# One 128-partition load for the shifted values, gate rows patched from Pool's queue, and a new issue order

## Chip, cores, metric

The kernel runs on one core of a Trainium2 chip. The metric is the device time of one execution in microseconds, lower is better. Before the change the median was 159.94 us over four runs (157.32 to 165.34).

Executions of one kernel vary by a few per cent here. A run over 1.5% above the fastest of the same kernel is called slow, and ratios are taken from fast runs alone.

## The reference

A layer norm, then two branches on the same normalised rows: a sliding attention with 32 heads of 20 channels, where each position looks at 8 keys that lie 2 apart, and a gate, in which a router picks 2 of the 2048 rows, an expert MLP changes those two, and a SiLU of the result multiplies the attention output.

```python
def reference(A_x, A_wqkv, A_wo, B_x, B_w_r, B_w_gate, B_w_up, B_w_down):   # cut
    x = A_x                                  # (1, 2048, 640) bf16
    xn = _layernorm(x, axis=-1)
    # A: W, dil = 8, 2;  idx = pos[:, None] - arange(W) * dil, masked where negative
    #    logits = q . k[idx] * scale; attn = softmax(logits); o = attn . v[idx]; s = o @ wo
    # B: r = xn @ w_r; idx = argsort(-r)[:, :2]; y = (silu(xs @ w_gate) * (xs @ w_up)) @ w_down
    #    y *= sigmoid(r[idx]); upd = scatter_add(0, idx, y); returns xn + upd
    s = _A_ref(xn, A_wqkv, A_wo)
    g = _silu(_B_ref(xn, B_w_r, B_w_gate, B_w_up, B_w_down))
    return x + s * g
```

## The kernel before

The sequence is worked in four stages of 512 positions. The values of a stage go to a scratch in device memory (`vd`) and come back as `vsh`, where partition 32·w4 + h holds head h shifted by 2·w4 positions. VectorE multiplies them with the attention weights (`av`), TensorE sums the products. There is one `vsh` for all stages, so a part of it can be loaded for the next stage only when this stage's product has read it.

```python
def load_wo(dd):                              # four loads of 32 partitions
    src = bass.AP(A_wo.tensor, A_wo.offset + dd * D, [[DH * D, H], [4 * D, G5], [1, D]])
    nc.sync.dma_start(wo[32 * dd:32 * (dd + 1), :, :], src)

def v_load(j, g0, ng):                        # called with (0, 2), (2, 2), (4, 1): 12 DMAs a stage
    n = (4 * ng - 1) * VR + ST + 8            # 4202 or 2098 elements a row
    for w4 in range(4):
        src = bass.AP(vd[j].tensor, vd[j].offset + 4 * g0 * VR + HALO - 8 - DIL * w4, [[DH * VR, H], [1, n]])
        nc.sync.dma_start(vsh[32 * w4:32 * (w4 + 1), 4 * g0 * VR:4 * g0 * VR + n], src)

def av(j, u):                                 # cut: one product over a part of vsh
    nc.vector.tensor_tensor(out=dst, in0=attn..., in1=vv, op=ALU.mult)

def gate_out():                               # the two 128-row tiles that hold the picked rows, to scratch
    for k in range(2):
        src, dst = gate_tile(k)
        nc.sync.dma_start(out=dst, in_=src)
def gate_rows():                              # the two new rows into the scratch
    for k in range(2):
        nc.sync.dma_start(out=zd[bass.ds(regs[k], 1), :]..., in_=grow[k:P:32, :])
def gate_back():                              # and the tiles back
    for k in range(2):
        dst, src = gate_tile(k)
        nc.sync.dma_start(out=dst, in_=src)

# ... cut; every engine runs its own steps in the order of one hand-made list, ORDER:
# zo, zw, zi = gate_out, gate_rows, gate_back; vs = store values; vl = load vsh; y = av;
# cm = combine (result times gate); od = add it to the output
for name in ORDER.split():
    step[name]()
```

All of these DMAs but the `od` ones of the first three stages (Pool's queue) stand on the sync queue, which issues them in this order. While one of them waited, none behind it was issued: in the trace of the kernel before, the second of `zo` waited 8.5 us for the first, and the vsh loads behind it went out from 99.9 us on only.

## Time and profile before

| | before |
|---|---|
| median of 4 runs | 159.94 us |
| profiled execution (slow) | 163.1 us span, granted clock 0.93 |
| TensorE (PE) / VectorE (DVE) / ScalarE (ACT) busy | 83% / 75% / 67% |

Lines of the page of the kernel before: busy time, the DMA engines' busy tenths in 40 slices, the chain of waits that ended last, one group of instructions (busy us, mean ns, idle time before it and what ended it), and one group of DMA issues (count, KB each, median us from issue to landing).

```profile
span 163.1 us, 3011 instructions
...
PE 135.0 (83%) x1159; PEld 66.9 (41%) x1179; DVE 122.0 (75%) x118; ACT 108.6 (67%) x201; POOL 17.7 (11%) x77
...
DMA  5899994098999033999995862993668999921175
...
PE 54%; DMA 27%; ACT 5%; DVE 5%; SPq 4%; issue 2%; DVEq 0%
PE pp L284 31%; PE so L421 9%; DMA vsh<-vd 8%; DMA wg<-in_B_w_gate_dram 7%; DMA zd<-grow 5%; PE lg L333 4%; DMA vd<-v_sb 3%; PE oa L407 3%; PE tp L274 3%; DMA z<-in_A_x_dram 2%; SPq L314 2%; DMA z<-zd 2%; DVE ss L467 1%; SPq L486 1%; DVE pr
...
L392 DVE TENSOR_TENSOR prod<-attn,vsh 128x8192 bf16<-128x8192 bf16 (+3 forms) x14 | 44.6, 3202 | 13.4 <-DMA vsh<-vd 13.1
...
vsh<-vd SPq DMA_DIRECT2D x32, 262.6 KB, 8.5
```

TensorE rules the first two thirds. VectorE's product L392 sat idle 13.4 us, nearly all of it for vsh, and all of that after 110 us, in the tail of the kernel. A 262.6 KB load takes 8.5 us at the median, with several in flight.

Windows of the kernel before (start and end; length; busy us and count of each engine; granted clock, DMA share of 16 engines, GB/s; up to 20 packet records are open at once in the first window, so that a share can read above 1). The first, second and last windows hold mostly vsh loads, the third wg (weights, 128 rows), the fourth mostly wd (weights, 108 rows).

```profile
core 0: us, PE busy (x) PEld busy (x) DVE busy (x) ACT busy (x) POOL busy (x), PEclk, DMA share, GB/s
43.00:51.00 8.00, 7.88 (x73) 4.69 (x77) 8.00 (x7) 7.96 (x15) 0.00 (x0) 1.00 1.02 224
64.00:76.00 12.00, 11.89 (x100) 5.40 (x100) 9.81 (x13) 9.97 (x15) 3.76 (x3) 1.00 1.00 225
80.50:82.50 2.00, 2.00 (x11) 0.91 (x10) 2.00 (x1) 1.07 (x2) 0.00 (x0) 1.00 1.10 342
92.00:96.00 4.00, 3.95 (x33) 2.27 (x33) 3.83 (x6) 3.93 (x7) 0.00 (x0) 1.00 0.83 237
126.00:138.00 12.00, 6.85 (x60) 2.96 (x61) 6.63 (x5) 4.89 (x9) 2.34 (x2) 0.76 1.04 235
```

Two things to read. With the DMA engines full (shares of 1.00 to 1.10), vsh loads move only 224 to 235 GB/s, wg 342. And wd's 108-row loads keep the engines 83% busy from 92 to 96 us. No record names the engine of a packet; the count of engines is read from such shares.

What the sync queue waited for in the kernel before (us in total, times, longest), then pieces of its chain of waits (start, length, what):

```profile
SPq L314 <- DMA vd<-v_sb: 12.0, 3, 4.3
...
SPq L593 <- DMA zd<-z: 8.5, 1, 8.5
SPq L597 <- DMA zd<-grow: 7.9, 1, 7.9
...
SPq L602 <- DMA z<-zd: 1.8, 1, 1.8
```

```profile
104.54 8.60 DMA zd<-grow
...
116.11 2.54 DMA z<-zd
...
119.08 5.30 DMA vd<-v_sb
...
125.77 5.89 DMA vsh<-vd
...
131.68 7.66 DMA vsh<-vd
```

The row patches of the gate hold the sync queue from 104.5 us; the last stage's value store is issued at 119.1 only, and its shifted loads land at 139.

### The profile page before, as it was taken

The numbers are of one execution on the slowest core, as the hardware profiler recorded it, in microseconds if no ns is written. First come the engines' busy times: TensorE is split into PE (matmuls) and PEld (weight loads), VectorE is DVE, ScalarE is ACT, GpSimd is POOL, SyncE is SP. The second block draws the span as 40 slices with busy tenths as digits, with TensorE's granted clock in tenths as the row PEclk, the third lists the DMA queues.
The fourth block names the chain that finished last, engine by engine and source line by source line (L and its number), as shares of the span: only waits on it lengthen the run. The fifth ranks groups of instructions, "written<-read, shape, count | busy, mean of one in ns | idle before, by whom it ended". The sixth has DMA issues, their size and how long they took to land.

```text
span 163.1 us, 3011 instructions
## 1 busy us (share of the span) xinstructions
PE 135.0 (83%) x1159; PEld 66.9 (41%) x1179; DVE 122.0 (75%) x118; ACT 108.6 (67%) x201; POOL 17.7 (11%) x77
## 2 busy tenths in 40 slices
PE   6779999999999999999969999993199619499630
PEld 2256545434455434444424636341063303165410
DVE  1635299999999999599988898932799365794930
ACT  3987998998799999977679879954025721145100
POOL 7880000000000000161000000000000303000110
PEclk9969999999999999999999999999659975969995
DMA  5899994098999033999995862993668999921175
GB/s 152 209 375 368 302 329 155 10 316 214 285 227 305 16 131 111 245 206 214 333 330 142 256 200 73 227 225 62 172 182 242 220 234 242 191 41 44 41 127 114
DMA packets 18958, 32.08 MB, mean 197 GB/s; under 512 B 2192, under 2 KB 16720, under 8 KB 17872
## 3 DMA queue, kind: packets, MB, share of 16 engines
q1 hardware_dynamic: 17072, 29.60, 67.0%
q0 software_dynamic: 1584, 1.97, 7.6%
q10 hardware_dynamic: 288, 0.33, 0.6%
q8 instruction: 9, 0.15, 0.4%
q14 instruction: 5, 0.04, 0.1%
HBM read 26.24 MB, written 7.61 MB: 208 GB/s over the span
## 4 chain that ended last, share of the span: by engine, by line
PE 54%; DMA 27%; ACT 5%; DVE 5%; SPq 4%; issue 2%; DVEq 0%
PE pp L284 31%; PE so L421 9%; DMA vsh<-vd 8%; DMA wg<-in_B_w_gate_dram 7%; DMA zd<-grow 5%; PE lg L333 4%; DMA vd<-v_sb 3%; PE oa L407 3%; PE tp L274 3%; DMA z<-in_A_x_dram 2%; SPq L314 2%; DMA z<-zd 2%; DVE ss L467 1%; SPq L486 1%; DVE prod L392 1%
## 5 line engine op out<-in xcount | busy, mean ns | idle before, releaser
L284 PE MATMUL pp<-xnT,wqkv 128*128 128x512 bf16 (+1 forms) x302 | 68.6, 373 | 0.7
L392 DVE TENSOR_TENSOR prod<-attn,vsh 128x8192 bf16<-128x8192 bf16 (+3 forms) x14 | 44.6, 3202 | 13.4 <-DMA vsh<-vd 13.1
L322 DVE TENSOR_TENSOR prod<-q_sb,k_sb 128x4096 bf16<-128x4096 bf16 (+1 forms) x14 | 44.4, 3193 | 2.8 <-ACT k_sb L299 2.4
L284 PEld LDWEIGHTS <-wqkv 128*128 128x128 bf16 x315 | 30.2, 99 | 33.8 <-issue 3.2
L421 PE MATMUL so<-wo,o_sb 128*128 128x128 bf16 (+1 forms) x153 | 27.5, 339 | 2.4 <-DVE ss L467 1.4
L407 PE MATMUL oa<-prod,sall 128*32 128x512 bf16 (+2 forms) x240 | 12.7, 327 | 12.5 <-DVE prod L392 11.6
L421 PEld LDWEIGHTS <-o_sb 128*128 128x128 bf16 x160 | 14.7, 114 | 14.6 <-issue 7.5
L441 ACT CAST ss<-so 128x512 bf16<-128x512 f32 x12 | 7.0, 601 | 17.0 <-PE so L421 10.6
L417 ACT CAST o_sb<-oa 128x512 bf16<-128x512 f32 (+2 forms) x22 | 11.8, 564 | 7.2 <-PE oa L407 4.8
L292 ACT ACTIVATE q_sb<-pp 128x512 bf16<-128x512 f32 (+1 forms) x23 | 12.4, 545 | 4.4 <-PE pp L284 4.4
L299 ACT CAST v_sb<-pp 128x512 bf16<-128x512 f32 x20 | 11.6, 589 | 4.2 <-PE pp L284 4.0
L458 POOL DMA_DIRECT2D out_dram<-ss x3 | 4.0, 1341 | 77.3 <-DVE ss L455 77.3
L407 PEld LDWEIGHTS <-sall 128*32 128x32 bf16 x240 | 4.9, 98 | 18.4 <-issue 9.5
L247 DVE BATCH_NORM_STATS2 st<-z 128x6 f32<-128x320 bf16 x16 | 7.0, 478 | 6.7 <-DMA z<-in_A_x_dram 6.7
L299 ACT CAST k_sb<-pp 128x512 bf16<-128x512 f32 x20 | 11.4, 588 | 0.5 <-PE pp L284 0.5
L278 ACT COPY xnT<-tp 128x640 bf16<-128x640 bf16 x16 | 10.5, 705 | 0.7 <-PE tp L274 0.7
L333 PE MATMUL lg<-prod,ind 128*32 128x512 bf16 x160 | 10.2, 380 | 0.1
L476 ACT ACTIVATE z<-z 128x1280 bf16<-128x1280 bf16 x8 | 10.3, 1285 | 0.0
L162 ACT ACT_TABLE_LOAD x7 | 9.0, 1283 | 1.9 <-PEq L696 1.8
L274 PE MATMUL tp<-ident,z 128*128 128x128 bf16 x80 | 7.2, 231 | 2.0 <-DVE z L268 2.0
L274 PEld LDWEIGHTS <-z 128*128 128x128 bf16 x80 | 5.5, 103 | 5.5 <-DVE z L268 2.9
L268 DVE TENSOR_SCALAR z<-z,mv,rstd 128x640 bf16<-128x640 bf16 x16 | 6.5, 454 | 1.0 <-ACT rstd L264 1.0
(88 smaller groups left out, 103.4 us busy)
## 6 DMA issues: line engine op xcount, KB each, us to landing
vsh<-vd SPq DMA_DIRECT2D x32, 262.6 KB, 8.5
vd<-v_sb SPq DMA_DIRECT2D x4, 657.5 KB, 4.3
wqkv<-in_A_wqkv_dram SPq DMA_DIRECT2D x3, 800.0 KB, 8.6
wu<-in_B_w_up_dram SPq DMA_DIRECT2D x5, 432.0 KB
wg<-in_B_w_gate_dram SPq DMA_DIRECT2D x5, 432.0 KB, 10.7
wd<-in_B_w_down_dram SPq DMA_DIRECT2D x4, 540.0 KB
vsh<-vd SPq DMA_DIRECT2D x16, 131.1 KB, 3.0
z<-in_A_x_dram SPq DMA_DIRECT2D x3, 640.0 KB, 12.2
```

The lines of the kernel that those rows point to most:

```text
L274: nc.tensor.transpose(tp[:, k5, :], z[:, i, P * k5:P * (k5 + 1)], ident[:])
L278: nc.scalar.copy(xnT[:, :, P * i:P * (i + 1)], acc.pop(("t", i))[:])
L284: nc.tensor.matmul(pp[:], lhsT=wqkv[:, k5, col:col + P], rhs=xnT[:, k5, ST * j + t0:ST * j + t0 + n], start=(k5 == 0), stop=(k5 == KD - 1))
L292: nc.scalar.activation(out=dst, in_=pp[:], func=ACT.Copy, scale=SCALE)
L299: nc.scalar.copy(dst, pp[:])
L322: nc.vector.tensor_tensor(out=dst, in0=q_sb[:, s0:s0 + n, :].unsqueeze(2).to_broadcast([P, n, W, ST]), in1=kv, op=ALU.mult)
L333: nc.tensor.matmul(lg[32 * w4:32 * (w4 + 1), w2, :], lhsT=ind5[:, g, :], rhs=prod[:, a:a + ST], start=(g == 0), stop=(g == G5 - 1), tile_p ...
L392: nc.vector.tensor_tensor(out=dst, in0=attn[:, :, t0:t0 + n].unsqueeze(2).to_broadcast([P, 2, 4 * ng, n]), in1=vv, op=ALU.mult)
L407: nc.tensor.matmul(oa[32 * dd:32 * (dd + 1), i, :], lhsT=sall[:, 0:32], rhs=prod[:, a:a + n], start=(w2 == 0), stop=(w2 == 1), tile_positi ...
L417: nc.scalar.copy(o_sb[:, s0:s0 + m, t0:t0 + n], acc.pop(("o", j, g, t0))[:])
L421: nc.tensor.matmul(dst, lhsT=o_sb[:, o_slot(j, g), P * c:P * (c + 1)], rhs=wo[:, g, n0:n1], start=(g == 0), stop=(g == G5 - 1))
L476: nc.scalar.activation(out=z[:, 2 * h:2 * h + 2, :], in_=z[:, 2 * h:2 * h + 2, :], func=ACT.Silu)
```

## The change

Four things. (V) The four loads of a group pair become one of 128 partitions, with the shifts numbered the other way round so that the source steps forward. Its evident intent is fewer issues and a destination that reaches every partition. (W) The wo weights are loaded by group, in the same form. (G) The six gate DMAs go to Pool's queue, over two scratch copies, each of which gets both rows. (O) All steps are put in a new order.

```diff
-    zd = dram.tile([S, D], BF, name="zd")
+    zd = [dram.tile([S, D], BF, name=f"zd{k}") for k in range(2)]
@@ load_wo, one per group g
-        src = bass.AP(A_wo.tensor, A_wo.offset + dd * D, [[DH * D, H], [4 * D, G5], [1, D]])
-        nc.sync.dma_start(wo[32 * dd:32 * (dd + 1), :, :], src)
+        src = bass.AP(A_wo.tensor, A_wo.offset + 4 * g * D, [[D, 4], [DH * D, H], [1, D]])
+        nc.sync.dma_start(wo[:, g, :], src)
@@ v_load
-        for w4 in range(4):
-            src = bass.AP(vd[j].tensor, vd[j].offset + 4 * g0 * VR + HALO - 8 - DIL * w4, [[DH * VR, H], [1, n]])
-            nc.sync.dma_start(vsh[32 * w4:32 * (w4 + 1), 4 * g0 * VR:4 * g0 * VR + n], src)
+        off, dst = vd[j].offset + 4 * g0 * VR + HALO - 8 - 3 * DIL, vsh[:, 4 * g0 * VR:4 * g0 * VR + n]
+        src = bass.AP(vd[j].tensor, off, [[DIL, 4], [DH * VR, H], [1, n]])
+        nc.sync.dma_start(dst, src)
@@ gate_out and gate_back: nc.sync -> nc.gpsimd, zd -> zd[k]; gate_rows:
-            nc.sync.dma_start(out=zd[bass.ds(regs[k], 1), :]..., in_=grow[k:P:32, :])
+            for i in range(2):
+                nc.gpsimd.dma_start(out=zd[k][bass.ds(regs[i], 1), :]..., in_=grow[i:P:32, :])
@@ cut: const_mask and qk_reduce number the shifts 3 - w4; ORDER is a new list
```

More of the change, by code (lines that the diff above doesn't have):

```diff
@@ L51 @@
 ORDER = """
-x01d x03d x00d in x02d xw ls00 wq bi bs wk ls01 lp00 bm ls03 lv01 ls02 lz00 lv03 bh lp01 lp02 W lp03 t00 bn lz01
-te00 t01 te01 xd1 lz03 lz02 wv ls12 xd2 t03 te03 t02 q00a q02a q01a te02 k01 q02b q00ae q02ae k04 q01ae ls13
-q02be k01e q00b k00 k04e mu1 mu0 q00be q01b ls11 q01be wo2 k03 k02 q03 v01 ls10 lv11 lv13 lp1 lz12 q04 k00e lz11
-t12 lz13 xd3 v00 k03e k02e wo0 lz10 ls23 t10 q03e x00 v01e x01 ls20 x02 t13 q04e r00 x03 te12 te10 lv23 r01 t11
-v00e te13 te11 v04 v04e v03 wo3 pr0 ls21 v02 k11 ls22 x04 ls32 q13 v02e v03e ls31 k12 r02 lv21 ls30 r03 k11e
@@ L57 @@
-q13e ls33 r04 k13 lp2 k12e q12 k10 br lz23 lb0 mu3 lz22 mx0 lv31 q12e lz20 vs0 k13e q10 pr2 lz21 t23 k10e lv33
-q10e lp3 te23 ng0 t20 k14 q11 te20 q11e k14e x11 lz33 vh1 vl02 mu2 mu4 v13 lz31 lz30 v13e t22 lz32 q14 te22 v10
-t33 x10 ex0 dn0 q14e v10e x12 lg0 te33 t21 v11 t32 te21 v11e t31 sb0 v12 t30 te32 r10 at0 r11 v12e te30 te31
-vl00 vl01 r12 rt g00 y00 v14 pr1 q24 rte k22 m8 k24 g31 mi v14e rr lb1 kh k22e o000 vs1 q22 k20 mx1 g11 q30 q24e
-k24e q22e q21 o000e g01 y02 vl12 vl10 q30e y01 q20 rm ng1 k21 vh2 vl11 ix q21e k20e k23 v22 q20e g20 o001 o011
@@ L62 @@
-h1 ex1 o010 k21e dn1 q23 o011e v22e x20 k23e o010e lg1 q23e x21 ml v23 sb1 v23e q32 q31 at1 o020 q31e r20 v20
-q32e o001e o020e v20e v21 v21e y10 v24 k30 mg3 v24e k30e g10 k31 x22 mg2 mg0 mg4 mg1 h0 r21 hs vs2 o101 k31e hb
-g30 r22 o100 wo1 k32 s00 s03 ht o100e s02 s04 y11 g21 md3 s00e md0 md1 lb2 k32e o101e mx2 md2 zo ng2 vl21 s03e
-s02e s04e ex2 q33 s01 k33 dn2 lg2 y12 hc o111 x30 q33e yp vl20 o110 s01e k33e o111e q34 sb2 v30 k34 zr x31 o120
-r30 q34e at2 v31 zw v33 v34 k34e x32 y20 v32 o110e vh3 r31 v30e vl22 v33e v31e o120e r32 o201 s12 v34e zi y22
@@ L67 @@
-s14 s10 v32e vs3 lb3 s12e o201e mx3 xr vl30 y21 s14e ng3 vl32 ex3 s10e o200 o220 s11 dn3 cm0 od0 lg3 sb3 at3 y30
-s13 o210 o200e o211 o300 s11e o220e o210e y32 s13e vl31 cm1 o211e s20 s21 o300e y31 s20e o310 s21e o320 s24 s23
-o320e o310e od1 s30 y33 y34 cm30 o330 o331 s22 s31 s23e o340 o330e o331e o341 s22e s24e s32 cm31 od30 cm2 od2
-cm32 o340e o341e s33 od31 od32 cm33 od33
+x00d in x01d x02d ls00 x03d xw wq bm bh bi ls02 xd1 ls01 W lp00 lz00 lv01 ls03 wk t00 lv03 bn lp01 wo0 lp02 lp03
+lz01 lz02 te00 bs br t01 te01 t02 te02 lz03 t03 q02a te03 q01a ls12 q00b q03 k02 q02ae q01ae ls11 q02b q00be
@@ new lines @@
+q03e k02e lv11 q02be ls13 k00 q00a k01 lv13 ls10 q00ae k00e k01e lp1 wo4 lz10 wv xd2 lz13 v03 k03 v01 v04 ls20
+v03e ls21 q01b t13 v01e v02 k03e v04e xd3 mu1 te13 q01be lv21 t10 lz11 lz12 x00 k04 t11 v02e v00 te10 k04e te11
+t12 q04 te12 x01 v00e q10 pr2 pr0 mu4 wo2 q04e x02 q12 q13 k12 vs0 x04 ls31 q10e pr1 x03 ls23 r00 q13e r01 r02
+k12e r03 r04 v13 k13 vh1 ls33 lv31 k14 lv23 ls22 ls32 lp2 lz23 q12e lb0 ls30 lv33 v13e v10 mx0 k13e lp3 lz22 k10
+v10e k14e lz20 k10e t23 wo1 mu0 ng0 t22 lz33 lz30 te23 vl02 lz32 v14 mu3 k11 ex0 lz21 te22 lz31 x11 v14e q11
@@ new lines @@
+vl00 t33 dn0 t21 k11e q11e q14 t30 te33 te21 lg0 q14e t20 te30 vl01 sb0 v12 te20 t31 v11 x10 at0 t32 x12 v12e
+r10 te31 v11e r11 te32 rt y00 g30 r12 rte lb1 g00 m8 k21 k21e k20 mi k22 k23 wo3 q30 k20e g11 o000 o001 mu2 v22
+q24 vs1 vl10 k22e vh2 q20 q21 y01 g21 rr k23e mx1 q30e v22e rm ix ng1 q23 kh y02 g10 o001e v23 o020 o011 o000e
+h1 vl11 vl12 q20e ml o010 q24e q21e ex1 v23e dn1 o020e q22 q23e o011e o010e mg1 mg2 mg4 q22e mg0 k24 k24e v21
+mg3 v20 v21e lg1 x20 sb1 q31 x21 v20e q31e at1 v24 q32 r20 r21 x22 r22 h0 k32 v24e g01 q32e y10 hs lb2 k32e hb
@@ new lines @@
+q33 s01 vs2 mx2 md2 s03 k30 q33e g20 s01e ht s03e s04 g31 s00 y11 ng2 s04e md1 vh3 s00e ex2 s02 md3 k31 o101 md0
+k31e k30e o100 dn2 y12 k33 o100e vl22 hc x30 yp o110 lg2 o111 sb2 o101e k33e v33 v31 s02e zo v30 zr x31 at2 r30
+v30e o110e v33e k34 v32 v31e vl20 o111e v32e v34 y20 v34e zw k34e vl21 q34 o120 q34e r31 o120e o201 s10 x32 r32
+s14 s11 zi vs3 s13 s10e s14e s12 lb3 y21 mx3 cm0 xr o201e y22 o211 o210 vl30 ng3 s11e s12e o211e s13e ex3 o210e
+dn3 lg3 cm1 sb3 at3 o220 o200 o220e vl31 o200e y30 y31 s21 s24 o300 o310 vl32 s24e y32 s21e s22 o300e od0 s20
@@ L71 @@
+o310e s23 o320 o320e y34 o340 o341 o340e s30 s22e o341e s23e s20e y33 cm30 o330 o331 s33 cm2 cm33 od1 od33 s31
+cm31 o330e o331e s32 od31 od30 cm32 od2 od32
 """
@@ L181, in load_w, with load_wo @@
         eng.dma_start(wqkv[:, :, which * D:(which + 1) * D], wq_v[:, :, which * D:(which + 1) * D])
-    def load_wo(dd):
-        src = bass.AP(A_wo.tensor, A_wo.offset + dd * D, [[DH * D, H], [4 * D, G5], [1, D]])
-        nc.sync.dma_start(wo[32 * dd:32 * (dd + 1), :, :], src)
+    def load_wo(g):
+        src = bass.AP(A_wo.tensor, A_wo.offset + 4 * g * D, [[D, 4], [DH * D, H], [1, D]])
+        nc.sync.dma_start(wo[:, g, :], src)
     def load_wr():
@@ L227, in const_mask @@
         for w in range(1, W):
-            w4, w2 = w % 4, w // 4
+            w4, w2 = 3 - w % 4, w // 4
             nc.gpsimd.memset(mask[32 * w4:32 * (w4 + 1), w2, 0:DIL * w], NEG)
@@ L331, in qk_reduce @@
                 for w4 in range(4):
-                    a = SLOT * g + ST * (w4 + 4 * w2)
+                    a = SLOT * g + ST * (3 - w4 + 4 * w2)
                     nc.tensor.matmul(lg[32 * w4:32 * (w4 + 1), w2, :], lhsT=ind5[:, g, :], rhs=prod[:, a:a + ST],
@@ L532, in route_rows @@
         for k in range(2):
-            regs[k] = v = nc.values_load(ii[0:1, k:k + 1], engines=[ENG.Pool, ENG.SP], min_val=0, max_val=S - 1)
+            regs[k] = v = nc.values_load(ii[0:1, k:k + 1], engines=[ENG.Pool], min_val=0, max_val=S - 1)
             nc.gpsimd.tensor_copy(xs[:, :, k:k + 1], xnT[:, :, bass.ds(v, 1)])
@@ L587, in gate_tile @@
         t = regs[k] // P
-        return z[:, bass.ds(t, 1), :].rearrange("p a d -> p (a d)"), zd[bass.ds(t * P, P), :]
+        return z[:, bass.ds(t, 1), :].rearrange("p a d -> p (a d)"), zd[k][bass.ds(t * P, P), :]
     def gate_out():
@@ L592, in gate_out @@
             src, dst = gate_tile(k)
-            nc.sync.dma_start(out=dst, in_=src)
+            nc.gpsimd.dma_start(out=dst, in_=src)
     def gate_rows():
         for k in range(2):
-            nc.sync.dma_start(out=zd[bass.ds(regs[k], 1), :].rearrange("a (q n) -> (a q) n", q=4), in_=grow[k:P:32, :])
+            for i in range(2):
+                nc.gpsimd.dma_start(out=zd[k][bass.ds(regs[i], 1), :].rearrange("a (q n) -> (a q) n", q=4),
+                                    in_=grow[i:P:32, :])
     def gate_back():
@@ L601, in gate_back @@
             dst, src = gate_tile(k)
-            nc.sync.dma_start(out=dst, in_=src)
+            nc.gpsimd.dma_start(out=dst, in_=src)
     step = {"W": lambda: warm_up(NWARM), "in": init_small, "bi": const_ident, "bn": const_ind, "bs": const_sall,
@@ L615, in _build @@
         add(f"w{n}", load_w, nc.sync, i)
-    for dd in range(4):
-        add(f"wo{dd}", load_wo, dd)
+    for g in range(G5):
+        add(f"wo{g}", load_wo, g)
     for k5 in range(KD):
```

## The prediction

> **What bounds the kernel now.** The profiled execution spans 163.1 us (slow state, clock 0.93; the three times are 157 to 165). The page gives PE 83%, DVE 75%, ACT 67%: PE rules up to about 98 us, and from there the wait for shifted values rules. In the list of waits DVE's product prod<-attn,vsh waits 13.1 us for DMA vsh<-vd. In the chain of waits the sync queue stands at 101 to 132 us: 8.6 us for zd<-grow, then z<-zd, then the value store vd (issued only at 119.1), then 13.6 us of vsh loads. By windows, PE is busy 11.9 of 12 us (86 to 98) but 16.6 of 27 (113 to 140).
>
> **What the change takes away.** (a) The gate rows' six DMAs leave the sync queue for Pool's: the sync queue stood about 8.5 + 7.9 + 1.8 us in them. Alone: 6 to 10 us, by issuing the last stage's vsh loads sooner. (b) Forty-eight vsh issues of 0.42 us become twelve, mostly off the path. (c) The new order moves no work between engines; I give it about nothing.
>
> **What it adds.** The shape of the new loads. Before, both sides of a vsh load start with 32 rows. Now the source starts with 4 (four shifts, then 32 heads), the destination with 128. [...] the 108-row wd loads [...] run at a DMA share of 0.77 to 0.83 (88.5 to 96 us), the 128-row wg loads at 1.10 and 342 GB/s. [...]
>
> Estimate: one four-row-group load is 4 x 262.6 KB; over 4 engines 269 KB each. At wg's rate (342/16 = 21 GB/s an engine) that is 12.6 us; at the rate at which vsh loads run now (224 GB/s at a share of 1.02, 43 to 51 us, 14 GB/s an engine) 19 us. A stage needs two and a half: 31 to 48 us, against some 12 before. Four stages make 126 to 192 us of those four engines, from about 37 us on; with the other loads' shares (about 25 us) and the last stage's tail (about 17 us) the end is at 205 to 270 us. wg is queued behind stage 1's loads, so PE will stand at the expert product too.
>
> **Prediction.** If four engines: 190 to 275 us. If the loads spread over all 16 after all (a quarter): about 153 us[...]. Together 228 us, 8 in 10 within 152 to 275. Faster by over 2%: 0.22; within 2%: 0.03; slower: 0.75.
>
> **What would show it.** Right: median landing of vsh loads 12 to 20 us; DMA share about 0.25 in long stretches with under 100 GB/s; DVE's wait for vsh 50 us or more; PE waiting for wg at the expert product. No zd in the chain of waits. Wrong: vsh landing in 3 to 6 us at a share near 1.
>
> **What would make it wrong.** The loads are spread after all; an engine alone on its rows runs faster than 21 GB/s (then nearer 185); Pool's queue delays the gate rows so that the last combine waits for them.

The four engines are to be read as a supposition of the author's, and what is worked out from them as an estimate that hangs on it. The sum with four engines came to 205 to 270 us (126 to 192 us of loads from about 37 us on, 25 us of other loads, 17 us of tail), was widened to 190 to 275, and was blended with the 153 us to 228.

## More of the kernel before

The kernel before was run again beside every group of experiments; its fast runs had a mean of 157.9 us beside the changed kernel and of 160.7, 162.5 and 160.7 us beside the three groups. Differences of 2 or 3% between runs of different groups are to be taken with care.

## The result

The changed kernel takes 226.44 us (median of 4, 226.14 to 233.84), against 159.94 us. The ratio is 1.433 (95% interval 1.420 to 1.447). A ratio here is the mean time of one kernel's fast runs over that of the other's of the same rounds, so it is not quite the ratio of the medians quoted beside it. The result is correct.

The same lines of the page of the changed kernel (fast; the profile of before is a slow one, so the gap between them is a little understated):

```profile
span 224.8 us, 2972 instructions
...
PE 141.2 (63%) x1162; PEld 66.5 (30%) x1179; DVE 122.1 (54%) x118; ACT 109.1 (49%) x201; POOL 24.4 (11%) x85
...
DMA  5999567322722122222984822545324932220037
...
DMA 63%; DVE 15%; PE 11%; issue 7%; SPq 2%; POOLq 1%; ACT 1%; POOL 0%; DVEq 0%
DMA vsh<-vd 44%; DVE prod L392 10%; DMA cv<-top 8%; PE pp L284 7%; DMA wqkv<-in_A_wqkv_dram 5%; DMA wr<-in_B_w_r_dram 3%; DMA vd<-v_sb 2%; DVE ss L467 1%; PE so L421 1%; SPq L314 1%; PE hp L543 1%; DVE ss L455 1%; DVE m L348 1%; PE tp L274 
...
L392 DVE TENSOR_TENSOR prod<-attn,vsh 128x8192 bf16<-128x8192 bf16 (+3 forms) x14 | 44.6, 3203 | 55.4 <-DMA vsh<-vd 54.6
L407 PE MATMUL oa<-prod,sall 128*32 128x512 bf16 (+2 forms) x240 | 15.8, 399 | 54.2 <-DVE prod L392 54.0
...
vsh<-vd SPq DMA_DIRECT2D x8, 1050.5 KB
...
vsh<-vd SPq DMA_DIRECT2D x4, 524.5 KB
```

Busy times of DVE and ACT hardly changed and PE's rose by 6 us; nearly all of the loss is waiting. VectorE's product waits 54.6 us for vsh where it waited 13.1, TensorE's sums 54.0 us for that product. The vsh loads are 44% of the chain. The row of DMA tenths shows long stretches of 2.

Windows of the changed kernel in which vsh loads run nearly alone (columns as before), then DVE's longest waits, then the long pieces of the chain of waits:

```profile
47.00:55.00 8.00, 7.95 (x101) 4.78 (x104) 7.84 (x3) 7.75 (x13) 0.00 (x0) 1.00 0.26 95
80.00:102.00 22.00, 8.26 (x38) 2.57 (x36) 6.79 (x12) 6.92 (x11) 4.44 (x1) 0.66 0.25 83
132.00:142.00 10.00, 9.95 (x142) 5.12 (x143) 7.71 (x2) 8.25 (x13) 1.25 (x3) 1.00 0.26 85
182.00:204.00 22.00, 3.71 (x36) 1.86 (x37) 4.58 (x2) 1.56 (x3) 0.00 (x0) 0.50 0.26 87
```

```profile
DVE prod L392 <- DMA vsh<-vd: 54.6, 7, 11.8
DVE t L522 <- DMA cv<-top: 18.3, 1, 18.3
```

```profile
30.59 5.57 DMA vd<-v_sb
...
37.89 33.04 DMA vsh<-vd
...
76.43 18.55 DMA cv<-top
...
130.16 33.03 DMA vsh<-vd
...
172.73 33.16 DMA vsh<-vd
```

A share of 0.25 to 0.26 is what 4 busy engines of 16 give; 3.3 to 3.9 packets of vsh were in flight (below). From the issue of a stage's last load to its landing it takes some 33 us (it stands behind the others of its stage); all packets of a stage are through in 31 to 39 us where 12.6 to 16.3 us sufficed before, pauses between them included. The second wait was not foreseen: `cv<-top`, a row of the router of a hundred bytes, is issued on the same queue right behind the first load of stage 1 and lands 18.55 us after its issue, and VectorE runs nothing for 18.3 us until it is there. No zd is left in the chain.

The packet records of the traces give the vsh loads themselves (packets of 8404 and 4196 bytes; each line one stage's 2.69 MB, from first packet to last; of the kernel before, the fastest of its four stages):

```
changed   39.2 to  70.5: 31.3 us,  86 GB/s, 3.7 packets in flight, mean 352 ns per 8404-byte packet
changed   77.1 to 111.4: 34.2 us,  79 GB/s, 3.9 in flight, 419 ns
changed  130.3 to 162.7: 32.4 us,  83 GB/s, 3.8 in flight, 365 ns
changed  166.6 to 205.5: 38.9 us,  69 GB/s, 3.3 in flight, 411 ns
before    64.0 to  76.6: 12.6 us, 213 GB/s, 14.9 in flight, 614 ns
```

The four bursts of the changed kernel take 136.8 us in sum. With 39.2 us ahead of the first, gaps of 6.6 + 18.9 + 3.9 = 29.4 us between them and 19.3 us after the last, that is the whole span.

### The profile page after: what moved, and what is told of

The parts are those of the page before. It is cut to its first block, busy times and chain, and to the rows that moved or that the text cites. A ratio compares the mean times of both kernels' runs of the same rounds, so it can differ in the third digit from the quotient of the medians.

```text
span 224.8 us, 2972 instructions
## 1 busy us (share of the span) xinstructions
PE 141.2 (63%) x1162; PEld 66.5 (30%) x1179; DVE 122.1 (54%) x118; ACT 109.1 (49%) x201; POOL 24.4 (11%) x85
## 4 chain that ended last, share of the span: by engine, by line
DMA 63%; DVE 15%; PE 11%; issue 7%; SPq 2%; POOLq 1%; ACT 1%; POOL 0%; DVEq 0%
DMA vsh<-vd 44%; DVE prod L392 10%; DMA cv<-top 8%; PE pp L284 7%; DMA wqkv<-in_A_wqkv_dram 5%; DMA wr<-in_B_w_r_dram 3%; DMA vd<-v_sb 2%; DVE ss L467 1%; PE so L421 1%; SPq L314 1%; PE hp L543 1%; DVE ss L455 1%; DVE m L348 1%; PE tp L274 1%; DVE m L347 0%
## 5 line engine op out<-in xcount | busy, mean ns | idle before, releaser
L284 PE MATMUL pp<-xnT,wqkv 128*128 128x512 bf16 (+1 forms) x304 | 71.3, 382 | 12.3 <-ACT k_sb L299 8.7
L392 DVE TENSOR_TENSOR prod<-attn,vsh 128x8192 bf16<-128x8192 bf16 (+3 forms) x14 | 44.6, 3203 | 55.4 <-DMA vsh<-vd 54.6
L407 PE MATMUL oa<-prod,sall 128*32 128x512 bf16 (+2 forms) x240 | 15.8, 399 | 54.2 <-DVE prod L392 54.0
L421 PE MATMUL so<-wo,o_sb 128*128 128x512 bf16 (+1 forms) x154 | 25.9, 322 | 3.6 <-DVE ss L467 2.1
L407 PEld LDWEIGHTS <-sall 128*32 128x32 bf16 x240 | 5.8, 108 | 60.8 <-issue 43.1
L421 PEld LDWEIGHTS <-o_sb 128*128 128x128 bf16 x160 | 13.1, 105 | 16.6 <-issue 8.0
L534 POOL COPY xs<-xnT 128x5 bf16 x2 | 5.7, 2868 | 85.5 <-issue 85.5
L441 ACT CAST ss<-so 128x512 bf16<-128x512 f32 x12 | 6.9, 597 | 15.8 <-PE so L421 15.8
L443 ACT CAST ss<-so 128x512 bf16<-128x512 f32 x3 | 1.8, 586 | 20.3 <-DMA out_dram<-ss 17.6
L522 DVE MAX8 t<-cv 1x8 f32<-1x32 f32 x1 | 0.2, 182 | 18.3 <-DMA cv<-top 18.3
```

The costliest lines, as they stand in the source:

```text
L284: nc.tensor.matmul(pp[:], lhsT=wqkv[:, k5, col:col + P], rhs=xnT[:, k5, ST * j + t0:ST * j + t0 + n], start=(k5 == 0), stop=(k5 == KD - 1))
L392: nc.vector.tensor_tensor(out=dst, in0=attn[:, :, t0:t0 + n].unsqueeze(2).to_broadcast([P, 2, 4 * ng, n]), in1=vv, op=ALU.mult)
L407: nc.tensor.matmul(oa[32 * dd:32 * (dd + 1), i, :], lhsT=sall[:, 0:32], rhs=prod[:, a:a + n], start=(w2 == 0), stop=(w2 == 1), tile_positi ...
L421: nc.tensor.matmul(dst, lhsT=o_sb[:, o_slot(j, g), P * c:P * (c + 1)], rhs=wo[:, g, n0:n1], start=(g == 0), stop=(g == G5 - 1))
```

## The experiments

Theory: the one load uses only 4 DMA engines (the share of 0.25), because its source begins with a dimension of 4. First rival: the new order, or the gate rows on Pool's queue, costs the time. Second rival: one large load is slow whatever its split, because it lands as a whole. The first four ran on one chip, the next four on another, the last four on the first chip again, each with its own runs of the kernel before.

### e1: the changed kernel with four loads again

```diff
-        src = bass.AP(vd[j].tensor, off, [[DIL, 4], [DH * VR, H], [1, n]])
-        nc.sync.dma_start(dst, src)
+        for w4 in range(4):
+            off = vd[j].offset + 4 * g0 * VR + HALO - 8 - DIL * (3 - w4)
+            src = bass.AP(vd[j].tensor, off, [[DH * VR, H], [1, n]])
+            nc.sync.dma_start(vsh[32 * w4:32 * (w4 + 1), 4 * g0 * VR:4 * g0 * VR + n], src)
```

> The changed kernel with its vsh loads split again into four of 32 rows; all else (order, Pool gate rows, wo shape) stays. Theory (the one load uses 4 of 16 DMA engines): the whole loss goes; 148 to 162 us, packets of 8404 bytes back from about 320 ns to about 600 ns each with 16 in flight. Rival (the new order or the gate rows on Pool's queue cost the time): stays above 200 us.

Measured: 167.38 us, ratio 1.041 (1.035 to 1.047) to before; correct. Packets of 8404 bytes took 603 to 623 ns in the mean of a stage, with 10.5 to 13.8 in flight in the first three stages and 8.3 in the last, whose loads have a pause between them. So nine tenths of the loss are gone (1.433 to 1.041) and the first rival falls. The time is above the range that the theory gave, though: some 4% belongs to W, G or O, which I had put at nothing or at a gain. This 4% is less certain than its interval: only three of the seven runs of the kernel before in this group were fast, and by the medians (163.13 us) it is 2.6%.

DVE's waits in this run (the product's line is now 393, the early combine 456), and Pool's timeline (start, length, what, idle before and what ended it; L594 tiles out, L599 row patches, L605 tiles back):

```profile
DVE ss L456 <- DMA z<-zd: 9.5, 1, 9.5
...
DVE t L523 <- DMA cv<-top: 2.2, 1, 2.2
```

```profile
100.07 1.39 POOL L594 DMA_DIRECT2D zd<-z  x2 [19.87 <-ACT z L477]
109.55 0.59 POOL L599 DMA_DIRECT2D zd<-grow  x1 [8.08 <-ACT grow L585]
118.18 1.14 POOL L599 DMA_DIRECT2D zd<-grow  x2 [8.04 <-DMA zd<-grow]
123.34 0.54 POOL L599 DMA_DIRECT2D zd<-grow  x1 [4.02 <-DMA zd<-grow]
124.19 0.59 POOL L605 DMA_DIRECT2D z<-zd  x1 [0.31 <-issue]
131.38 0.57 POOL L605 DMA_DIRECT2D z<-zd  x1 [6.60 <-DMA z<-zd]
```

The row patches on Pool's queue wait for one another: from the first at 109.55 to the last tile's way back at 131.38 and on to its landing it is some 26 us, for which the combine (step cm0, which stands ahead of the last stage's products on DVE) waits 9.5 us. The router's row, stuck for 18.3 us in the changed kernel, waits 2.2 us here.

### e2: the kernel before with the one load alone

The edit is the `v_load` hunk of the change, with the shifts numbered 3 - w4 in const_mask and qk_reduce.

> The kernel before with only the one-DMA load and the mirrored shift numbering. Theory: the loss appears whole, 215 to 250 us, DMA share near 0.25 in the long waits. Rival (order or Pool queue): within 5% of before, about 160 us.

Measured: 242.57 us, ratio 1.506 (1.486 to 1.526); correct. V alone brings the whole loss, and more of it than all four parts together: with slow loads, the old order holds other DMAs on the sync queue as well. In the page of e2, the gate rows (zd<-grow) are 10% of the chain of waits, the issue of wg (L486) another 10%, and TensorE's expert product waits 22.5 us for wg:

```profile
DMA vsh<-vd 29%; SPq L486 10%; DMA zd<-grow 10%; PE pp L284 7%; PE so L421 6%; DVE prod L392 6%; DMA vd<-v_sb 5%; DMA wg<-in_B_w_gate_dram 4%; PE oa L407 2%; PE lg L333 1%; DMA z<-in_A_x_dram 1%; PE hp L543 1%; ACT L162 1%; ACT junk L253 1%
...
L543 PE MATMUL hp<-wg,xs 128*32 128x433 bf16 x20 | 2.2, 556 | 22.5 <-DMA wg<-in_B_w_gate_dram 22.5
```

V is sufficient.

### e3 and e4: the same one load, its source split 8 x 16 and 16 x 8

```diff
-        src = bass.AP(vd[j].tensor, off, [[DIL, 4], [DH * VR, H], [1, n]])
+        src = bass.AP(vd[j].tensor, off, [[DIL, 8], [DH * VR, 16], [1, n]])    # e3
+        src = bass.AP(vd[j].tensor, off, [[DIL, 16], [DH * VR, 8], [1, n]])    # e4
```

The values are wrong; bytes, number of rows, row length, destination and the number of DMAs are those of the changed kernel, and no branch depends on the values. What also differs is which rows of the scratch are read: those of 16 heads in e3 and of 8 in e4, in place of 32.

> The changed kernel with the source of its one load written as 8 x 16 rows in place of 4 x 32 (same bytes, same destination, wrong values on purpose). Theory: 8 engines, half the time per load, about 13 us for a stage's loads in place of 26; 165 to 190 us. Rival (one load of 128 rows is slow whatever its split, because it lands as a whole): about 226 us.

> As the last, with the source as 16 x 8 rows (wrong values on purpose). Theory: 16 engines in flight, 148 to 162 us[...]. Rival: about 226 us.

Measured: e3 196.57 us, ratio 1.211 (1.189 to 1.234); e4 166.04 us, ratio 1.029 (1.015 to 1.043). Windows of e3 (a slow profile) and of e4 in a stretch of vsh loads:

```profile
78.00:98.00 20.00, 11.34 (x77) 4.03 (x76) 7.81 (x12) 6.83 (x11) 5.94 (x3) 0.67 0.53 115
```

```profile
68.00:75.00 7.00, 4.25 (x31) 1.34 (x28) 6.83 (x9) 5.92 (x10) 5.00 (x1) 1.00 0.94 211
```

The share goes 0.25, 0.53, 0.94 with an outer dimension of 4, 8 and 16. The second rival falls: one load of 128 rows is as fast as four of 32 (166.04 us, e1 167.38) once its source begins with 16. The outer dimension of the source is the cause. (That the rows read were others does not explain it: e1 reads the same rows as the changed kernel and is about as fast as e4.) The dose is not quite what I expected, though: e3 was to halve a stage's loads to about 13 us and came in above its range, because they took 24 to 27 us. Twice the engines moved only 1.4 times the bytes a second (112 against 79 GB/s in stage 1), as each packet took 608 ns in the mean in place of 419. e4's time, too, is above the range given, by the same 3 to 4% as e1's.

### e5: the kernel before with the gate rows on Pool's queue

The edit is the zd and gate hunks of the change alone.

> The kernel before with only the gate rows moved to Pool's queue with two scratch copies; its own order. My recorded estimate: 6 to 10 us faster than before, because the sync queue no longer stands in them. Rival, from the four-load run: Pool's chain of row patches is longer (26 us there against 17 us on the sync queue) and a combine on DVE waits for it; then same or slower, 0 to +6 us.

Measured: 159.95 us against 162.92 us, but one fast run only (156.79 us; the fast runs of before were 161.2 to 163.5), so no ratio. Inconclusive, on the side of a small gain. DVE's combine waits 4.6 us for the tiles there, so the wait has moved from the sync queue to VectorE in part.

### e6, e7, e8: what the 4% of e1 are

e6 is e1 with the gate rows back on the sync queue, with one scratch copy; e7 is e1 with each wo load as four of 32 rows; e8 is e1 with the four loads in another order:

```diff
+        for dd in range(4):                                                       # e7, load_wo
+            src = bass.AP(A_wo.tensor, A_wo.offset + (4 * g + dd) * D, [[DH * D, H], [1, D]])
+            nc.sync.dma_start(wo[32 * dd:32 * (dd + 1), g, :], src)
-        for w4 in range(4):                                                       # e8, v_load
+        for w4 in (0, 2, 1, 3):
```

> The four-load run (167 us) with the gate rows back on the sync queue and one scratch copy; new order and wo shape stay. If the gate rows on Pool cost the four-load run its 4%: 158 to 164 us. If the new order does: 165 us or more.

> The four-load run with each wo load split into four of 32 rows as well, so that no load is held to 4 engines. If the 4-engine wo loads in front of the value weights cost something at the start: 2 to 3 us less than 167 us (PE loses about 2.4 us between 10 and 20 us there). If not: 167 us, or more by the longer issue of 20 loads in place of 5.

> The four-load run with the four 32-row loads issued in the order 0, 2, 1, 3, so that neighbours in the queue go to different halves of the partitions. [...] mean packet under 550 ns and 2 to 5 us less than 167 us. [...]

The "4-engine wo loads" of e7 are read from the trace of the changed kernel: the wo load (128 packets of 1280 bytes) that runs almost alone there, from 27.2 to 29.5 us, has a DMA share of 0.22 and moves 84 GB/s.

Measured: e6 167.67 us, ratio 1.030 (1.021 to 1.038); e7 164.26 us, 1.008 (0.998 to 1.017); e8 162.37 us, 0.998 (0.990 to 1.006). So putting the gate rows back does not give the 4% back: DVE's wait of 9.5 us for the tiles is gone in e6, and vsh loads are late in its place (waits of 6.0 us). The wo shape is worth 2% (by the medians, 3.1 us) to 3% (by ratios), the 2 to 3 us of its expectation or somewhat more; but not where it said: PE's busy time from 0 to 20 us did not rise (14.1 us, e1 14.6), while stage 0's shifted loads were through at 53.2 us in place of 56.8. e7 and e6 ran beside each other, e1 on another chip, so this goes by ratios. The alternating order gave packets of 538 to 556 ns in place of 603 to 623, just about the level expected, and 3% (by the medians) to 4% (by ratios) of the time.

These two gains can't be added. At DVE's copy of hT (the expert's hidden row), which starts at 103.5 us in e1 and 103.1 in e6, e7 is ahead of e1 by 4.7 us already, and e8 by 5.2: both win the same stretch, and neither has the wait of 2.2 us for the router's row. e12 below, which has both edits, is ahead by 2.3 us there. So how the 4% of e1 are shared out stays open; what is shown is that with either edit the kernel is within 2% of the kernel before.

### e9 to e12: towards a better version

e9 is the kernel before with the order 0, 2, 1, 3 and nothing else. e10 adds the gate rows on Pool's queue. e11 moves `cm0 od0` behind `y31` in the order, lets the row loop run outside the copy loop, and keeps stage 2's results in the projection weights, which are dead by then. e12 is the changed kernel with e7's wo loads, the alternating four loads, and the same mending for `cm0 od0` (behind y31) and `cm1 od1` (behind y32). The build with a third buffer for the results failed, hence the dead weights.

```diff
-            for i in range(2):          # gate_rows in e11 and e12: i outside, k inside
+        for i in range(2):
+            for k in range(2):
+        if ("ss", j) not in acc and j == NST - 2:
+            acc["ss", j] = wqkv[:, 0:TPS, 0:D]
```

> The kernel before with its four 32-row vsh loads issued in the order 0, 2, 1, 3 and nothing else. The alternating order took 5 us off the four-load run and its packets from about 620 to about 550 ns. If the gain belongs to the loads: 1 to 3% faster than before. If it belonged to the new order's slack: within 1%.

> The last with the gate rows on Pool's queue and two scratch copies. If the two gains add: 2 to 5% faster than before. If the combine's wait for the Pool chain eats it: no better than the alternate order alone.

> The last with what showed as its wait taken away: stage 0's combine stands behind two of the last stage's products on DVE (stage 2's results get their own room in the dead projection weights, so nothing waits for the buffer), and the row patches go round the copies first. If the 4.6 us wait of DVE for z<-zd was on the path: 3 to 6 us under the last run. If DVE then waits for vsh in the same place: within 1.5 us of it.

> The changed kernel with all three mended: four 32-row vsh loads in the order 0, 2, 1, 3, four 32-row wo loads each, and both early combines moved behind the last stage's products. If the 8.8 us wait for z<-zd was on the path of the alternate run (162 us): 153 to 158 us, faster than before. If not: 160 us or more.

Measured, beside 161.28 us of before (its fast runs 160.2 to 162.0): e9 159.35 us, e10 160.75 us, e11 159.10 us, e12 157.36 us. All are correct. e9 and e10 have one fast run of six (156.03 and 155.27 us), e11 two (156.82 and 155.43 us), so there is no ratio for them: each one's fast runs lie below all of before's, but whether the gains of alternation, Pool queue and later combine add is not shown. e12 has five fast runs and a ratio of 0.977 (0.971 to 0.983): it is faster than the kernel before by some 2% (whether by over 2% is unclear), and than the changed one by 69 us. DVE's waits for TensorE's sums and for vsh from 110 us on in e12 (a slow profile of 157.4 us); no wait for z<-zd is listed any more:

```profile
DVE prod L394 <- PE oa L409: 3.0, 1, 3.0
...
DVE prod L394 <- DMA vsh<-vd: 1.4, 1, 1.4
```

That the wait for z<-zd was worth its full 8.8 us is not shown: e12 differs from e8 in the wo loads too. It was run on another chip.

## Why the prediction was right

It forecast 228 us, slower with 0.75, on the ground of four engines; 226.44 us was measured. That ground, the engines, the share and the wait of VectorE, was right, and e1 to e4 show it. That the number is met within 1% is luck: 228 was a blend of 190 to 275 us and of 153 us for the other case, and terms of the sum were off in both directions. Point by point:

- Four engines. Right. The vsh loads had a DMA share of 0.25 to 0.26 with a source that begins with 4 rows (changed kernel), of 0.53 with 8 (e3) and of 0.94 with 16 (e4). With the four loads of 32 rows it was 1.00 to 1.04 in the kernel before and 1.01 in e1 (64 to 73 us).
- "12.6 us ... 19 us" for a load of four row groups. Mis-sized at its slow end. Its 128 packets over four engines are 32 each; at the 352 to 419 ns of the four bursts that is an estimated 11.3 to 13.4 us. The faster end was about right; the slow end, taken from the 14 GB/s per engine of the old loads, did not apply: with four engines the packets were faster than the 557 to 614 ns of the old loads.
- "126 to 192 us of those four engines", with "about 25 us" for other loads and "about 17 us" of tail. Measured 136.8, 29.4 and 19.3 us. The middle term has the right size for a reason that is only half the stated one: other loads ran within the bursts as well, and the gaps are the waits of one stage for another (store landed, product done).
- "PE will stand at the expert product too", for wg. Wrong. Waits before the expert's products in the changed kernel:

```profile
  POOL xs L534: 2.6, 1
...
  DMA wg<-in_B_w_gate_dram: 0.9, 2
```

  wg held PE's side up by 0.9 us. What the slow loads did hold up was the router's row cv, 18.3 us, one step earlier in the same branch. I had looked for the large transfers behind the slow loads and not for the small ones. In the old order the forecast holds: in e2 TensorE waits 22.5 us for wg. So what was missed is what the other parts of the change do to this wait.
- "Alone: 6 to 10 us" for the gate rows. Not confirmed: e5's one fast run is some 5 us under before's, and e1 against e6 shows no gain at all. Beside the vsh loads, Pool's queue waited 4.0 and 8.0 us in e1 for a 1.2 KB row patch before it issued the next, and 5.3 and 5.7 us in the changed kernel; on the sync queue of the kernel before, one took 8.6 us.
- "The new order ... I give it about nothing", and the wo loads not costed. Right for the order, as far as shown: e7, with both kinds of loads mended and the new order and Pool's queue kept, is within 1.7% of before. The wo loads, the same form on a smaller scale, should have been costed: e1, which still has them, is 4.1% slower than before, e7 0.8% (how much of this is theirs stays open, see e8).
- "About 153 us" had all engines been used. Wrong: e4, with a share of 0.94, takes 166 us.

What stays open: why four engines run their packets in 321 to 331 ns at the median of a stage, and eight (e3) need 537 to 645 ns, sixteen (e4) 599 to 634 ns. 8404 bytes in 321 to 331 ns are 25 to 26 GB/s for an engine; over a stage's loads, pauses included, the changed kernel moved 69 to 86 GB/s with other loads beside them, e3 100 to 113 and the kernel before 165 to 213. The number of partitions that a load goes to does not tell these apart: the 32-row loads of before took 557 to 614 ns a packet in the mean of a stage, the 128-row load of e4 578 to 608 ns, and the 128-row load of the changed kernel 352 to 419 ns. Why the alternating order has shorter packets (538 to 556 ns in e8, 603 to 623 in e1) is not shown either. The reading side was not tested apart: e3 and e4 read other rows than e1.

## What to carry to other kernels

Before merging loads into one, look at the outermost dimension of the merged source, not only at the partitions of the destination: with a merged source of 4 x 32 rows the DMA share fell from 1.00 or more to 0.25, and the kernel's time rose by 51% with this edit alone (e2) and by 43% with the whole change, though rows and bytes stayed the same; with 8 x 16 rows the share was 0.53, with 16 x 8 it was 0.94. When a load gets slow, look at what stands behind it on the queue: the costliest of these may be a row of a hundred bytes, as here, where VectorE stood 18.3 us for it. And a chain of dependent small DMAs that leaves one queue for another is not gone; ask which engine waits for its end (in e1 VectorE, 9.5 us).
